# Three early expert pairs behind the first layer, and half items between the late pairs

## The chip, the cores and the metric

The kernel runs on one core of one Trainium2 chip. The time is the device time of one execution in microseconds (us). Profiled times are read from one recorded execution of the kernel. On this core TensorE (PE) does the matrix products, VectorE (DVE) and ScalarE (ACT) evict and split them, GpSimd (POOL) does some elementwise work and issues the indirect gathers and scatters, and SyncE (SP) issues all other transfers.

## What is computed

The reference is an attention, a dense two-layer network and a routed network, one after the other, on 4 x 576 = 2304 tokens of width 512:

```
attn = softmax(mask(q k^T / 8)) v          # 8 heads of 64, blocks of 64 causal
h    = x @ w_in                            # 512 -> 1024
s    = h * softmax(h);  ln = (s - mean) / sqrt(var + 1e-6) * g_ln
x    = ln @ w_out                          # 1024 -> 512
e    = argmax(x @ w_gate)                  # one expert of 8 for each token
y    = relu(x[e] @ w1[e]) @ w2[e]          # 512 -> 1024 -> 512
out  = y * softmax(x @ w_gate)[e] * sigmoid(x @ w_output_gate)[e]
```

A product that has to be as good as fp32 is made from fp16 halves: each operand is split into a high and a low part, and three products (high-high, high-low, low-high) are summed in PSUM. This is why each weight is loaded as fp32 and then split by ACT (high part, line 1370) and DVE (low part, line 1373) or POOL (lines 455 and 460).

## The kernel before, in words

The order of all instructions is written by a planner (class `Plan`). Every operation is put down with its engine, an estimated cost, the buffers and keys it reads and writes, and a priority; a lower number is more urgent. `run` then places operations one by one: for each engine it takes, among those that can start within 60 ns of the earliest, the one with the lowest priority, books buffers of a tag while it does so, and issues it. So priorities decide the order within the limits that data and free buffers set, and each engine then runs its instructions in that written order on the chip.

The attention is followed by the dense network ("layer 1", function `layer1`) in 18 tiles of 128 tokens. Tile t has priority L0 + L1 * t, so tile 16 has 96.91 and tile 17 has 101.25. Each makes its first product into the PSUM tile H (two banks, one buffer; lines 903 to 905), takes the maximum, exponential and norm (lines 917 to 948), transposes (960), makes its second product (988 to 990), writes its tokens to the DRAM tile `x2d` (1002), and makes the gate logits (1028 to 1030).

The routed network works on *items*. A *pair* is 256 tokens of one expert (two tiles of 128), a *half* is 64 tokens. There are NPAIR2 = 8 pairs, items 0 to 7, and NHALF = 5 halves, items 8 to 12; tokens that are left after these go to blocks that run only if they exist (`chain`, after everything else). An item of class `Slot` has these steps:

- `load_w`: four loads of 512 KB of the expert's w1 (line 1442, on SP) into raw buffers `w1f`. There are four of these, and w2 uses them too.
- `split_w`: eight splits into one of two buffers `w1s` (one for even, one for odd items).
- `load_x`: the token numbers (line 1420, on SP), then a gather of the tokens from `x2d` (line 1427, on POOL), one for each 128 tokens.
- `trans_x`: transposes on PE (1464) and a copy on DVE (1469) into the single buffer `gx`.
- `gemm1`, the first product: lines 1482 to 1484, 96 matmuls into the PSUM tag S (three banks), evicted by ACT (1508) and DVE (1511).
- `gemm2`, the second product: lines 1543 to 1545 for a pair, 24 matmuls for each of the two token tiles, evicted and scaled by ACT (1577) and scattered by POOL (1580); lines 1539 and 1540 for a half.

`fill_w2` loads and splits the w2 of one expert, four loads of 512 KB (line 1391). All eight experts' w2 stay in SBUF: the place of expert slot e lies over buffers of the attention and of layer 1, and can be written when those are done (`low{e}`; slot 2 lies over w_in, slot 7 over w_out). `last(j)` gives the highest expert slot that item j can belong to; the second product of item j waits for the w2 of all slots up to that one.

The first NEARLY = 2 pairs are *early*: their experts are chosen by `order` from the counts of the first EC = 14 tiles (`tab0`), while tiles 14 to 17 are still in work. All other items are chosen by `items` from all 18 tiles (`tab`), so they cannot be loaded or gathered before the last logits and the table are done. Early pairs, like all pairs, accumulate their second product in H; halves use H and A in turn. A is one PSUM bank, which the attention uses before.

The items' priorities are M0 + MJ * j with M0 = 99.05 and MJ = 14.54 for pairs, and 6 more for each half; they run in the order 0 to 12. The loads of w1 have 13 less, those of w2 12.1 less, those of x 17.5 less:

```
def pri_of(j):
    return M0 + MJ * min(j, NPAIR2) + MH * max(j - NPAIR2, 0)
```

Of the kernel before, what the change touches and what calls it, by code (L numbers as in the profile page):

```python
# [12 lines left out]
AF = mybir.ActivationFunctionType  # L13
ALU = mybir.AluOpType
# [5 lines left out]
P = 128  # L20
BLK = 64
# [163 lines left out]
def kernel(  # L185
# [15 lines left out]
    B, H, S, D = q.shape  # L201
# [17 lines left out]


    EC = 14
    NEARLY = 2
    NPAIR2 = 8
    NHALF = 5
    NITEM = NPAIR2 + NHALF
    NLATE = NPAIR2 - NEARLY
    NBLK = 10
# [6 lines left out]
    TLT = "T"  # L234
    RKT = "T"
    RP = 7.31
    TP = -0.41
    DP0 = -1.33
    DP1 = 2.98
    L0 = 27.47  # L240
    L1 = 4.34
    M0 = 99.05
    MJ = 14.54
    MH = 6.0
    MW = 13.0
    MF = 12.1
    MX = 17.5
    MT = 3.6
    FENG = ("dve", "pool", "dve", "dve")
    NPX = 2  # L250
    NPS = 3
# [56 lines left out]
    eb2 = const.tile([P, E], F32, name="eb2")  # L308
    tab0 = const.tile([1, E + 3 * NEARLY], I32, name="tab0")
    tab = const.tile([1, 4, NDYN], I32, name="tab")  # L310
# [41 lines left out]
    pln = Plan(SLK, AHEAD)  # L352
# [78 lines left out]
    op = pln.op  # L431
# [927 lines left out]
    def last(j):  # L1359
        if j < NEARLY:  # L1360
            return j
        return max(p for p in range(E) if p * (P * EC // E - BLK) <= 2 * P * j)
# [18 lines left out]
    def fill_w2(pl, e, pri):  # L1381
        ej = []
        for cc in range(F2C // 2):
            wf = Buf("w1f")
            sl = slice(2 * cc, 2 * cc + 2)

            def ld(wf=wf, cc=cc):
                if not ej:
                    ej.append(reg(tab0[0:1, e : e + 1], ET.SP, E - 1))
                src = w2[bass.ds(ej[0], 1), 2 * cc * P : (2 * cc + 2) * P, :]  # L1390
                nc.sync.dma_start(
                    out=wf.t.rearrange("p (c f) -> p c f", c=2),
                    in_=src.rearrange("o (c p) f -> p (o c) f", p=P))

            pl.op("sp", 900.0, ld, r=["top", "tab0"], w=[wf], pri=pri, lat=900.0, xfer=1456.0,
                  dly=1550.0)
            halves(
                pl, wf, lambda sl=sl: w2v[:, e, 0, sl].rearrange("p c f -> p (c f)"),
                lambda sl=sl: w2v[:, e, 1, sl].rearrange("p c f -> p (c f)"),
                ("w2", e, cc), SW2, pri, FENG[cc], [f"low{e}"])  # L1400

    class Slot:
# [121 lines left out]
            return rd + ([tab_of(self.j)] if self.j else [])  # L1524

        def gemm2(self, pl, pri):
            n, hh, hl, yp = self.n, self.hh, self.hl, Buf(self.out)
            where = []

            def mm(part, t):  # L1530
                if not where:
                    where.append(place(self.j))
                e, np_ = where[0]
                o = yp.t[:, t * 512 : (t + 1) * 512]
                ts_ = slice(t * P, (t + 1) * P)
                for f in range(2 * part, 2 * part + 2):
                    wh, wl = (w2v[:, 0:np_, a_, f, :][:, e] for a_ in range(2))
                    if n == BLK:
                        nc.tensor.matmul(o, hh.t[:, f, 0:P], wh, start=(f == 0), stop=False)
                        nc.tensor.matmul(  # L1540
                            o, hh.t[:, f, 0:P], wl, start=False, stop=(f == F2C - 1))
                        continue
                    nc.tensor.matmul(o, hh.t[:, f, ts_], wh, start=(f == 0), stop=False)  # L1543
                    nc.tensor.matmul(o, hh.t[:, f, ts_], wl, start=False, stop=False)  # L1544
                    nc.tensor.matmul(o, hl.t[:, f, ts_], wh, start=False, stop=(f == F2C - 1))  # L1545

            for t in range(self.nt):
                for part in range(4):
                    rd = self.w2_keys(part)
                    for f in range(2 * part, 2 * part + 2):  # L1550
                        rd += self.hidden(f)
                    pl.op("pe", (4 if n == BLK else 6) * c_mm(512),
                          lambda part=part, t=t: mm(part, t), r=rd, w=[(yp, t)], pri=pri)
                self.finish(pl, pri, yp, t)

        def finish(self, pl, pri, yp, t):
            y, m = self.y[t], self.m

            def scale():
                return self.ix.bitcast(F32)[0:m, t, 1:2]  # L1560

            if self.n == BLK:
                hl = self.hl

                def z():
                    return hl.t[0:BLK, 0:4].rearrange("p c t -> p (c t)").bitcast(F32)

                pl.op("act", c_act(512), lambda: nc.scalar.activation(
                    out=z(), in_=yp.t[BLK:P, 0:512], func=AF.Copy), r=[(yp, t)], w=[hl], pri=pri)
                pl.op("dve", c_dve(512), lambda: nc.vector.tensor_tensor(  # L1570
                    out=z(), in0=yp.t[0:BLK, 0:512], in1=z(), op=ALU.add), r=[(yp, t)], w=[hl],
                    pri=pri)
                pl.op("pool", c_pool(512), lambda: nc.gpsimd.tensor_scalar(
                    out=y.t[0:BLK], in0=z(), scalar1=scale(), scalar2=0.0, op0=ALU.mult,
                    op1=ALU.add), r=[hl, ("ix", self.at)], w=[y], pri=pri)
            else:
                pl.op("act", c_act(512, 1), lambda: nc.scalar.activation(  # L1577
                    out=y.t, in_=yp.t[:, t * 512 : (t + 1) * 512], func=AF.Copy, scale=scale()),
                    r=[(yp, t), ("ix", self.at)], w=[y], pri=pri)
            pl.op("pool", 1040.0, lambda: nc.gpsimd.indirect_dma_start(  # L1580
                out=out, out_offset=bass.IndirectOffsetOnAxis(
                    ap=self.ix[0:m, t, 0:1], axis=0),
                in_=y.t[0:m], in_offset=None, bounds_check=N - 1, oob_is_err=False),
                r=[y, ("ix", self.at)], w=["out"], pri=pri, lat=900.0,
                xfer=6.0 * m, dly=1690.0)
# [29 lines left out]
    for t in range(NT):  # L1615
# [3 lines left out]
        if t + 1 == EC:  # L1619
            table_consts(L0 + L1 * t - RP)  # L1620
            order(L0 + L1 * t - RP)
    items(L0 + L1 * NT + TP)
    pln.fence("top", LOW, TOP, area)
    for e in range(E):
        pln.fence(f"low{e}", e * W2E, (e + 1) * W2E, area)
    op("pool", 4000.0, lambda: [nc.gpsimd.memset(x[2], 0.0) for x in pln.tags["xg"]],
       r=["top"], w=["xgz"], pri=M0 - 10)

    def pri_of(j):
        return M0 + MJ * min(j, NPAIR2) + MH * max(j - NPAIR2, 0)  # L1630

    for e in range(E):
        fill_w2(pln, e, pri_of(next(j for j in range(NPAIR2 + 1) if last(j) >= e)) - MF)
    for j in range(NITEM):
        whole = j < NPAIR2
        sl = Slot(j, 2 * P if whole else BLK, j % 2, j,
                  "H" if whole or (j - NPAIR2) % 2 else "A")
        pri = pri_of(j)
        sl.load_w(pln, pri - MW)
        sl.split_w(pln, pri - MW)  # L1640
        sl.load_x(pln, pri - MX)
        sl.trans_x(pln, pri - MT)
        sl.gemm1(pln, pri)
        sl.gemm2(pln, pri)
    with tc.manual_schedule():
        setup_first()
        pln.run({"pool": 2000.0, "act": 1500.0, "dve": 1500.0, "sp": 500.0})
# [60 lines left out]
```

## Time and profile before

| What | Value |
|---|---|
| median of 3 runs | 781.38 us (776.32 to 785.42) |
| profiled execution | 781.41 us |
| its span, first to last instruction | 779.7 us |
| mean granted TensorE clock | 0.914 |
| PE busy | 611.7 us (78%) |
| DVE busy | 533.7 us (68%) |
| ACT busy | 367.5 us (47%) |
| POOL busy | 331.0 us (42%) |
| chain that ended last | PE 34%, DVE 29%, issue 12%, POOL 10%, DMA 9%, ACT 4% |

PE is the busiest engine, but its busy time is a mean over stages. The span has the attention up to about 410 us, with layer 1 beside it and after it up to 540 us, early pairs between 480 and 552 us, late pairs from 570 to 716 us and halves up to 764 us. The page's second part cuts the span into 40 slices of 19.5 us each, with one digit for each.

### The profile page before, as it was taken

The page shows a single profiled execution, that of the slowest core. Times are in us where ns is not written, and L with a number is a line of the kernel's source. Part 1 is how long each engine was busy: PE and PEld are TensorE (multiplying, and loading weights), DVE is VectorE, ACT ScalarE, POOL GpSimd, SP SyncE. Part 2 cuts the span into 40 slices and gives each one's busy share as a digit, 9 for nine tenths or more (in the row PEclk, how much of TensorE's full clock was granted, in tenths as well). Part 3 has the DMA queues.
Part 4 walks back from the last instruction along what each step waited for, and adds up shares of the span by engine and source line. Part 5 has one row for each costly group of instructions (what it writes and reads, how often), then busy time and mean ns, then how long its engine had stood idle before and what let it go on. Part 6 is the DMA issues. An engine that isn't in the chain of part 4 may idle for free.

```text
span 779.7 us, 14588 instructions
## 1 busy us (share of the span) xinstructions
PE 611.7 (78%) x5124; PEld 374.0 (48%) x5124; DVE 533.7 (68%) x1241; ACT 367.5 (47%) x871; POOL 331.0 (42%) x349
## 2 busy tenths in 40 slices
PE   2567767779997899897997765979269999999861
PEld 1445534434554455454553333746055667666530
DVE  6799999998997779877742746576964453234630
ACT  4558666535654555545532354556243533234510
POOL 6861757747355644535241234364442131221110
PEclk9759998979999999899998988899769999999986
DMA  8872847857988878675521167646397462343600
GB/s 208 193 203 69 177 106 163 174 130 160 206 172 145 169 161 177 131 156 85 109 52 28 27 203 260 173 162 229 110 321 240 153 207 98 132 149 136 224 9 19
DMA packets 207204, 117.46 MB, mean 151 GB/s; under 512 B 182928, under 2 KB 183056, under 8 KB 207120
## 3 DMA queue, kind: packets, MB, share of 16 engines
q1 hardware_dynamic: 203504, 106.94, 55.0%
q0 software_dynamic: 3616, 9.46, 3.3%
q8 instruction: 45, 0.74, 0.4%
q14 instruction: 39, 0.32, 0.2%
HBM read 71.49 MB, written 10.80 MB: 106 GB/s over the span
## 4 chain that ended last, share of the span: by engine, by line
PE 34%; DVE 29%; issue 12%; POOL 10%; DMA 9%; ACT 4%; SPq 0%; POOLq 0%; ACTq 0%; DVEq 0%
DVE mem L730 4%; DMA mem<-mem 4%; PE H L1543 3%; PE S L1482 3%; PE H L1545 3%; PE H L1544 3%; PE S L1484 3%; PE S L1483 3%; DVE mem L842 3%; PE S L988 2%; PE S L989 2%; PE S L990 2%; POOL mem L460 2%; DVE mem L1373 2%; DVE mem L777 2%
## 5 line engine op out<-in xcount | busy, mean ns | idle before, releaser
L1373 DVE SCALAR_TENSOR_TENSOR mem<-mem 128x1024 f16<-128x1024 f32 x76 | 99.9, 1347 | 22.6 <-ACT mem L1370 22.3
L460 POOL TENSOR_TENSOR mem<-mem 128x576 f16<-128x576 f32 (+2 forms) x70 | 104.1, 1495 | 15.5 <-ACT mem L580 8.7
L1370 ACT ACTIVATE mem<-mem 128x1024 f16<-128x1024 f32 x84 | 84.5, 1050 | 34.2 <-DMA mem<-in_moe_w_dram 28.5
L736 ACT ACTIVATE mem<-S,mem 128x512 f32<-128x512 f32 (+4 forms) x160 | 81.6, 515 | 37.1 <-DVE mem L730 26.7
L1482 PE MATMUL S<-mem 128*128 128x256 f16 (+1 forms) x416 | 85.6, 244 | 4.2 <-DVE mem L1469 3.3
L1484 PE MATMUL S<-mem 128*128 128x256 f16 (+1 forms) x416 | 85.5, 244 | 0.8 <-DVE mem L1373 0.8
L1483 PE MATMUL S<-mem 128*128 128x256 f16 (+1 forms) x416 | 85.5, 244 | 0.0
L455 POOL TENSOR_SCALAR mem<-mem 128x576 f16<-128x576 f32 (+2 forms) x65 | 54.6, 845 | 54.8 <-PE A L864 20.0
L730 DVE TENSOR_REDUCE mem<-S 128x1 f32<-128x512 f32 (+4 forms) x128 | 68.3, 543 | 5.9 <-PE S L718 3.0
L1580 POOL DMA_INDIRECT out_dram<-mem,ix x21 | 24.9, 1188 | 99.0 <-ACT mem L1577 78.7
L988 PE MATMUL S<-mem 128*128 128x512 f16 x144 | 58.0, 403 | 3.6 <-ACT mem L736 3.0
L903 PE MATMUL H<-mem 128*128 128x512 f16 x144 | 58.1, 403 | 0.7 <-DVE mem L930 0.7
L904 PE MATMUL H<-mem 128*128 128x512 f16 x144 | 58.0, 403 | 0.0
L989 PE MATMUL S<-mem 128*128 128x512 f16 x144 | 57.7, 401 | 0.0
L990 PE MATMUL S<-mem 128*128 128x512 f16 x144 | 57.4, 399 | 0.0
L905 PE MATMUL H<-mem 128*128 128x512 f16 x144 | 57.4, 398 | 0.0
L1511 DVE SCALAR_TENSOR_TENSOR mem<-S,mem 128x512 f16<-128x512 f32 x37 | 25.3, 689 | 46.4 <-ACT mem L1508 46.4
L830 PE MATMUL T<-idf,mem 128*128 128x128 f32 (+1 forms) x208 | 41.8, 304 | 16.6 <-DVE mem L842 10.1
L1543 PE MATMUL H<-mem 128*128 (+1 forms) x128 | 48.5, 379 | 7.9 <-ACT mem L1577 6.2
L715 PE MATMUL S<-mem 128*64 128x64 f16 (+4 forms) x160 | 47.4, 315 | 2.4 <-ACT mem L736 2.3
L1508 ACT ACTIVATE mem<-S 128x512 f16<-128x512 f32 x37 | 22.0, 597 | 57.8 <-PE S L1484 57.7
L1545 PE MATMUL H<-mem 128*128 (+1 forms) x128 | 48.5, 379 | 0.0
(189 smaller groups left out, 1705.5 us busy)
## 6 DMA issues: line engine op xcount, KB each, us to landing
mem<-in_moe_w_dram SPq DMA_DIRECT2D x84, 512.0 KB, 4.9
x2d<-mem SPq DMA_DIRECT2D x22, 256.0 KB, 3.1
mem<-in_q_dram SPq DMA_DIRECT2D x16, 288.0 KB, 3.5
mem<-in_k_dram SPq DMA_DIRECT2D x16, 288.0 KB, 3.9
mem<-in_v_dram SPq DMA_DIRECT2D x16, 288.0 KB, 3.6
mem<-mem SPq DMA_DIRECT2D x32, 144.0 KB, 2.9
mem<-in_moe_w_in_dram SPq DMA_DIRECT2D x8, 512.0 KB, 4.2
mem<-in_moe_w_out_dram SPq DMA_DIRECT2D x8, 512.0 KB, 4.0
```

The costliest lines, as they stand in the source:

```text
L460: nc.gpsimd.tensor_tensor(out=dst, in0=a, in1=b, op=ALU.subtract)
L730: nc.vector.tensor_reduce(out=stt.t[0:M, c : c + w], in_=src, op=ALU.max, axis=AX.X, negate=True)
L736: op("act", c_act(n, 1, 1), lambda: nc.scalar.activation(out=pexp.t[0:M, po : po + n], in_=pt.t[0:M, co : co + n], func=AF.Exp, bias=stt.t ...
L988: nc.tensor.matmul(x2p.t, lT.t[:, 0, f], wout[:, 0, f], start=(f == 0), stop=False)
L989: nc.tensor.matmul(x2p.t, lT.t[:, 0, f], wout[:, 1, f], start=False, stop=False)
L990: nc.tensor.matmul(x2p.t, lT.t[:, 1, f], wout[:, 0, f], start=False, stop=(f == FC - 1))
L1370: pl.op("act", c_act(1024, sb=1), lambda: nc.scalar.activation(out=hi(), in_=wf.t, func=AF.Copy, scale=sc), r=[wf, *x], w=[key + (0,)], pr ...
L1373: pl.op("dve", c_dve(1024), lambda: nc.vector.scalar_tensor_tensor(out=lo(), in0=wf.t, scalar=sc, in1=hi(), op0=ALU.mult, op1=ALU.subtract ...
L1482: nc.tensor.matmul(o, wh, xh, start=(c == 0), stop=False)
L1483: nc.tensor.matmul(o, wh, xl, start=False, stop=False)
L1484: nc.tensor.matmul(o, wl, xh, start=False, stop=(c == KC - 1))
L1543: nc.tensor.matmul(o, hh.t[:, f, ts_], wh, start=(f == 0), stop=False)
```

## The change

NEARLY becomes 3, so pairs 0 to 2 are early. Their second product goes to A, one bank, one token tile after the other (`yps` holds a buffer for each token tile), and no longer to H. M0 becomes 103, so that the products of all early pairs have a higher number than tile 17 of layer 1 (101.25); MJ becomes 8. The table of the late items gets a lower number (TP from -0.41 to -8). The items run in a written order, SEQ, in which the halves 8 to 11 stand in twos before the pairs 6 and 7, and half 12 comes last. The buffers `w1s` alternate along SEQ. Loads, splits and transposes get the priority of the item before (`prev`) and small offsets, in place of fixed ones.

```diff
-    NEARLY = 2
+    NEARLY = 3
...
-    TP = -0.41
+    TP = -8.0
...
-    M0 = 99.05
-    MJ = 14.54
-    MH = 6.0
-    MW = 13.0
-    MF = 12.1
-    MX = 17.5
-    MT = 3.6
+    M0 = 103.0
+    MJ = 8.0
+    MH = 3.0
+
+    SEQ = (0, 1, 2, 3, 4, 5, 8, 9, 6, 10, 11, 7, 12)
...
         def gemm2(self, pl, pri):
-            n, hh, hl, yp = self.n, self.hh, self.hl, Buf(self.out)
+            n, hh, hl = self.n, self.hh, self.hl
+            yps = [Buf(self.out) for _ in range(1 if self.out == "H" else self.nt)]
             where = []
+
+            def at(t):
+                if self.out == "H":
+                    return yps[0], slice(t * 512, (t + 1) * 512)
+                return yps[t], slice(0, 512)
...
-    def pri_of(j):
-        return M0 + MJ * min(j, NPAIR2) + MH * max(j - NPAIR2, 0)
-
+
+    at, prev = {}, {}
+    pri = M0
+    for s_, j in enumerate(SEQ):
+        at[j], prev[j] = pri, at[SEQ[s_ - 1]] if s_ else pri - MJ
+        pri += MJ if j < NPAIR2 else MH
     for e in range(E):
-        fill_w2(pln, e, pri_of(next(j for j in range(NPAIR2 + 1) if last(j) >= e)) - MF)
-    for j in range(NITEM):
+        j = next(j for j in range(NPAIR2 + 1) if last(j) >= e)
+        fill_w2(pln, e, prev[j] + 0.6)
+    for s_, j in enumerate(SEQ):
         whole = j < NPAIR2
-        sl = Slot(j, 2 * P if whole else BLK, j % 2, j,
-                  "H" if whole or (j - NPAIR2) % 2 else "A")
-        pri = pri_of(j)
-        sl.load_w(pln, pri - MW)
-        sl.split_w(pln, pri - MW)
-        sl.load_x(pln, pri - MX)
-        sl.trans_x(pln, pri - MT)
-        sl.gemm1(pln, pri)
-        sl.gemm2(pln, pri)
+        sl = Slot(j, 2 * P if whole else BLK, s_ % 2, j,
+                  "A" if j < NEARLY or not (whole or (j - NPAIR2) % 2) else "H")
+        sl.load_w(pln, prev[j] - MJ)
+        sl.split_w(pln, prev[j] + 0.3)
+        sl.load_x(pln, prev[j] - MJ)
+        sl.trans_x(pln, prev[j] + 0.2)
+        sl.gemm1(pln, at[j])
+        sl.gemm2(pln, at[j])
```

With the reference's inputs the tokens of the experts, counted from the reference in the order of the first 14 tiles, are 576, 448, 306, 206, 128, 64, 64 and 0 after 14 tiles, and 768, 512, 306, 270, 320, 64, 64 and 0 at the end.

## Rows read from the trace of the kernel before

**Rows 1.** The page's 40 slices: busy tenths of PE, its granted clock.

```profile
PE   2567767779997899897997765979269999999861
PEclk9759998979999999899998988899769999999986
```

**Rows 2.** Stretches: length, busy us of PE, PEld, DVE, ACT, POOL, clock, DMA, GB/s.

```profile
480.00:551.50 71.50, 63.18 (x429) 40.13 (x427) 47.20 (x89) 35.27 (x47) 37.50 (x28) 0.95 0.63 202
551.50:575.00 23.50, 3.60 (x32) 3.18 (x32) 18.59 (x60) 7.86 (x8) 12.97 (x10) 0.55 0.53 178
575.00:600.40 25.40, 22.81 (x150) 14.61 (x148) 15.83 (x17) 11.93 (x14) 3.40 (x4) 0.95 0.89 307
...
715.40:764.10 48.70, 38.36 (x593) 24.62 (x589) 21.66 (x25) 17.85 (x22) 8.12 (x9) 0.89 0.31 103
```

**Rows 3.** Waits of PE from 540 us: total us, times, longest.

```profile
PE T L1464 <- DMA mem<-x2d,ix: 19.9, 2, 19.0
PE A L1539 <- DVE mem L1469: 6.6, 2, 4.0
PE H L1543 <- ACT mem L1577: 5.4, 7, 0.8
PE A L1539 <- DVE mem L1511: 2.2, 1, 2.2
```

**Rows 4.** Timeline of PE, tile 17 and early pairs: start, us, instruction, [idle before].

```profile
481.85 0.27 PE L1482 MATMUL S<-mem 128*128 128x256 f16 x1
...
506.58 0.38 PE L905 MATMUL H<-mem 128*128 128x512 f16 x1
...
515.32 0.38 PE L1543 MATMUL H<-mem 128*128 128x512 f16 x1 [1.70 <-DVE mem L930]
...
522.73 0.38 PE L1543 MATMUL H<-mem 128*128 128x512 f16 x1 [0.78 <-ACT mem L1577]
...
551.12 0.38 PE L1545 MATMUL H<-mem 128*128 x1
```

**Rows 5.** Timeline, from the last logits to the first late pair.

```profile
539.95 0.17 PE L1030 MATMUL S<-wg,mem 128*128 128x16 f16 x1
...
561.09 0.20 DVE L1337 CAST tab<-mem 1x96 int32<-1x96 f32 x1
...
570.46 1.03 PE L1464 MATMUL T<-idh,mem 128*128 128x128 f16 x8 [18.96 <-DMA mem<-x2d,ix]
...
575.13 0.42 PE L1482 MATMUL S<-mem 128*128 128x256 f16 x1
```

**Rows 6.** Timeline of PE, starts of pairs 3, 5 and 6, and of pair 5's second product.

```profile
600.24 0.27 PE L1482 MATMUL S<-mem 128*128 128x256 f16 x1
...
647.17 0.27 PE L1482 MATMUL S<-mem 128*128 128x256 f16 x1 [0.34 <-DVE mem L1469]
...
657.65 0.38 PE L1543 MATMUL H<-mem 128*128 x1
...
670.33 0.27 PE L1482 MATMUL S<-mem 128*128 128x256 f16 x1 [0.33 <-DVE mem L1469]
```

**Rows 7.** Timeline of the halves: PE, and the last scatter on POOL.

```profile
729.84 0.19 PE L1482 MATMUL S<-mem 128*128 128x64 f16 x1
...
737.78 0.19 PE L1482 MATMUL S<-mem 128*128 128x64 f16 x1 [0.18 <-DVE mem L1469]
...
763.64 0.38 PE L1540 MATMUL A<-mem 128*128 x1
...
766.49 0.91 POOL L1580 DMA_INDIRECT out_dram<-mem,ix  x1 [0.28 <-POOL mem L1573]
```

**Rows 8.** Two stretches with weight loads, columns as in rows 2.

```profile
510.00:550.00 40.00, 36.75 (x239) 21.81 (x237) 28.83 (x49) 20.69 (x30) 23.03 (x16) 1.00 0.62 205
570.00:600.00 30.00, 26.01 (x175) 17.54 (x176) 20.75 (x20) 14.04 (x16) 7.93 (x6) 0.87 0.87 301
```

**Rows 9.** The page's DMA issues: times, size, median us to landing.

```profile
mem<-in_moe_w_dram SPq DMA_DIRECT2D x84, 512.0 KB, 4.9
```

More of the change, by code (lines that the diff above doesn't have):

```diff
@@ L1533, in mm @@
                 e, np_ = where[0]
-                o = yp.t[:, t * 512 : (t + 1) * 512]
+                yp, cols = at(t)
+                o = yp.t[:, cols]
                 ts_ = slice(t * P, (t + 1) * P)
@@ L1552, in gemm2, with finish @@
                     pl.op("pe", (4 if n == BLK else 6) * c_mm(512),
-                          lambda part=part, t=t: mm(part, t), r=rd, w=[(yp, t)], pri=pri)
-                self.finish(pl, pri, yp, t)
-        def finish(self, pl, pri, yp, t):
+                          lambda part=part, t=t: mm(part, t), r=rd, w=[(at(t)[0], t)], pri=pri)
+                self.finish(pl, pri, *at(t), t)
+        def finish(self, pl, pri, yp, cols, t):
             y, m = self.y[t], self.m
@@ L1568, in finish @@
                 pl.op("act", c_act(512), lambda: nc.scalar.activation(
-                    out=z(), in_=yp.t[BLK:P, 0:512], func=AF.Copy), r=[(yp, t)], w=[hl], pri=pri)
+                    out=z(), in_=yp.t[BLK:P, cols], func=AF.Copy), r=[(yp, t)], w=[hl], pri=pri)
                 pl.op("dve", c_dve(512), lambda: nc.vector.tensor_tensor(
-                    out=z(), in0=yp.t[0:BLK, 0:512], in1=z(), op=ALU.add), r=[(yp, t)], w=[hl],
+                    out=z(), in0=yp.t[0:BLK, cols], in1=z(), op=ALU.add), r=[(yp, t)], w=[hl],
                     pri=pri)
@@ L1577, in finish @@
                 pl.op("act", c_act(512, 1), lambda: nc.scalar.activation(
-                    out=y.t, in_=yp.t[:, t * 512 : (t + 1) * 512], func=AF.Copy, scale=scale()),
+                    out=y.t, in_=yp.t[:, cols], func=AF.Copy, scale=scale()),
                     r=[(yp, t), ("ix", self.at)], w=[y], pri=pri)
```

## The prediction

> **What bounds the kernel now.** I read the page's slices first [rows 1]: PE is busy for 7 to 9 tenths almost everywhere, but there is one slice of 2 late in the span, where the clock falls to 6 or 7 tenths, and a fall at the very end. The table by stages says what these are [rows 2]. Between 480 and 551.5 us PE does the tail of layer 1 and two early pairs and is 63.2 of 71.5 us busy. Then it has 3.6 us of work in 23.5 us. Then comes the first late pair, at 0.95 of the clock, and after 715.4 us the five halves take 48.7 us with 38.4 us of work. The list of PE's waits names the causes [rows 3]: 19.9 us for the gather of tokens (one wait of 19.0), and 6.6 + 2.2 us in the halves for copies and evictions that run late on DVE.
>
> The hole at 551.5 us is a chain of latencies. The last logits of tile 17 end at 539.95 + 0.17 = 540.1 us, the table of the late items is written at 561.09, the gathered tokens arrive at 570.46, the first late product starts at 575.13 [rows 5]: 35.0 us from logits to product. PE has only the rest of pair 1 to put against it, which ends at 551.12 + 0.38 = 551.5 [rows 4]. Outside this stretch and the halves, the late pairs are bound by PE alone: from pair 5 to pair 6 it is 670.33 - 647.17 = 23.16 us [rows 6], and the waits in that time are 0.78 and 0.33.
>
> **The third early pair.** It needs only the counts of 14 tiles, so its work can stand in the hole. The same work up to the end of pair 1 ends at 551.5 now; with one more pair of 23.16 us it ends at 574.7. Today the third pair ends, and pair 3 begins, at 600.24 [rows 6]. That is 600.2 - 574.7 = **-25.6**. It holds the gather wait, the half clock of pair 2's start (matmuls of 0.42 us against 0.27 [rows 5, 6]) and its waits for weights.
>
> Can the late items be ready at 574.7? Now tile 17's first product is cut in two: PE goes to pair 0 at 481.85, because 99.05 is below 101.25, and the last matmul of tile 17 ends at 506.58 + 0.38 = 507.0 [rows 4]. From there to the logits it is 33.1 us, and 35.0 to the first late product. With 103 for pair 0 the six matmuls that are missing can follow at 481.85, and the chain would end near 483 + 33 + 35 = 551. Even if nothing of this is gained it ends at 575, as now, where PE comes free. So the chain is covered with up to 23 us to spare. Against that spare go the steps moved ahead of it: one index load and four loads of 512 KB on SP, two gathers and two scatters on POOL, and eight splits (ACT and DVE). POOL is 37.5 and DVE 47.2 us busy in those 71.5 us [rows 2]; I take 0.
>
> The third pair's counts hold: its expert has 448 tokens after 14 tiles, so it is full. The five late pairs and five halves then cover the rest exactly, and the optional blocks stay empty, as now (the last scatter is at 766.49 [rows 7]).
>
> **Another accumulator.** Pair 0's second product waits 1.70 us for tile 17's eviction from H [rows 4]; in A this wait goes: **-1.7**. On the other side A has one bank, and the second token tile has to wait for the eviction of the first. With H the same wait is there, but only after six matmuls of the second tile: the product starts at 515.32 and stops at 522.73 - 0.78 = 521.95, after 30 matmuls at 0.22 us, 24 and 6 [rows 4]. Without those six it is 6 x 0.22 + 0.78 = 2.1 us. The bound is 0 to 1.3 us more for each early pair, 0 where PE has layer 1 or the first 36 matmuls of the next pair to put there, so 0 to 3.9. I take **+1.3**, for the pair at the end. The Trainium skill has a rule against this edit, in "PSUM — Partial Sum Buffer" (Summary: rules for kernel authors): while a result is read, let the matmuls write another bank. By that rule all three early pairs would pay, and the sum below would be 752.
>
> **The halves.** A half that is fed takes 737.78 - 729.84 = 7.94 us [rows 7]; five take 39.7 against 48.7 [rows 2], so 9.0 less. The weights of a half are 2 MB: at 301 GB/s [rows 8], 524288 / 301000 = 1.74 us for each of four loads, 7.0 us, which is what ties a row of halves to the loads now (waits of up to 4.0 us [rows 3]). A pair in between gives 23 us for the same loads. Two halves stand together twice, and the next item's `w1s` comes free only when the first of them has ended its first product; a wait of about half a microsecond at each of these two places I leave in. **-8.0**; bounds -9.0, and 0 if the waits only move.
>
> **The loads.** This is the unknown one. In the new numbers the w1 of item j + 1 stands ahead of the w2 that item j needs (119 against 119.6 for pair 4's w1 and slots 3 and 4). That w1 can be split only when the pair two before has ended its first product, and until then it holds all four raw buffers. A first product takes 657.65 - 647.17 = 10.5 us [rows 6], so pair 2's ends 23.2 - 10.5 = 12.7 us before 574.7, at 562. Eight loads (slots 3 and 4) follow, at 1.74 us, or at 524288 / 205000 = 2.56 us as beside layer 1 [rows 8], plus 4.9 us to land the last [rows 9], minus one load: 579 to 585. They are needed when pair 3's first product ends, 10.5 us after 574.7, at 585. Pair 4 with slots 5 and 6 repeats it 23 us later. So it just fits. Bounds: 0, and about 5 us at each of two places; I take **+2.0**.
>
> **The sum** goes against the profiled execution, 781.4 us (1.7 over its span, and equal to the median of the runs): 781.4 - 25.6 - 1.7 + 1.3 - 8.0 + 2.0 = **749.4**, so 749. The 15.7 us after the last matmul (779.7 - 764.0) stay.
>
> **The rivals.**
> - *The feed binds.* Loads go at 3.3 us in place of 2.6, since the splits on POOL are slow and DVE is shared: eight take 6 us more, at pairs 3 and 4. 749 + 12 = 761. For it: the DMA share is 0.87 to 0.89 whenever late pairs load now [rows 2, 8]. Against it: 205 GB/s is a rate that was held while layer 1 still used DVE.
> - *The hole moves.* The third pair's steps stretch layer 1's tail beyond its 23 us, or PE's written order puts something that waits before work that could run; the wait of 19 us comes back elsewhere, and the halves keep their waits: 749 + 19 + 8 = 776, no change. Against it: the chain may be as late as now at no cost.
> - *Slower: the raw buffers.* While w1 of a pair holds all four, no w2 arrives. If eight loads take more than the 23 us of a pair, every pair waits. The gain of 32 us is gone when pairs 3 and 4 wait 16 us each, with eight loads in 39 us, 4.9 us for each. At 6 us each it is two times 48 - 23 = 25, so 749 + 50 = 799. For it: the holding is in the order of priorities. Against it: no stretch of rows shows more than 2.6.
> - *Better.* Feed and halves cost nothing, and the short product waits are filled: 749.4 - 2.0 - 1.3 - 1.0 = 745, and less where layer 1's tail has fewer waits: 740.
> - *Not what it says:* a third pair that is not full would send tokens to the optional blocks, which run after everything, unhidden: half an item's 8 us, 7 of loads and a gather chain of some 10, 774. The counts exclude it for these inputs.
>
> **How the numbers follow.** Forecast 0.62; the feed 0.17; better 0.08; the hole moves 0.06; slower 0.06; optional blocks 0.01. A change under 1% (7.8 us) can't be told from none here, as the three runs span 9 us. Faster: 0.62 + 0.17 + 0.08 = 0.87; same: 0.06 + 0.01 = 0.07; slower 0.06. The range takes in the better case near its edge and the feed rival with a few us more: 738 to 767. What is left out is the other three and the tails, about 0.2.
>
> **What would show it.** PE without a gap over 3 us between 482 and the start of pair 3, with that start near 575 (the hole, right); tile 17's first product in one piece, logits near 520 (order); early second products into A with waits of at most 2.1 us; halves of about 8 us between pairs. Pair 3's or 4's second product waiting for a split of w2 by 5 us or more would show the feed; a wait of PE for a gather after the early pairs would show the hole moved. The prediction is wrong if pair 3 begins after 590, or if the items after it take more than 25 us for each pair.

## The result and the profile after

The changed kernel takes **755.35 us** (median of four runs, 753.55 to 761.62) against 782.21 us of the kernel before on the same chip: ratio 0.9679, 95% interval 0.9596 to 0.9762. The forecast was 749, with a range of 738 to 767. The recorded execution took 753.69 us, its span is 751.8 us.

The page's slices of the changed kernel, PE and its clock, answer to [rows 1]:

```profile
PE   2568858868988888989799776779899999999981
PEclk9998998698999899999999898999989999999995
```

The slice of 2 is gone, and so are the clock's 6 and 7 beside it. The stages of the changed kernel (length, busy us of PE, PEld, DVE, ACT, POOL, clock, DMA share, GB/s) answer to [rows 2]:

```profile
485.85:557.35 71.50, 61.45 (x435) 39.36 (x433) 52.97 (x142) 31.52 (x43) 31.68 (x26) 0.95 0.58 162
557.35:579.19 21.84, 21.84 (x156) 14.43 (x154) 15.61 (x16) 14.16 (x17) 8.62 (x7) 1.00 0.94 325
579.19:724.33 145.14, 137.02 (x1273) 93.78 (x1272) 80.78 (x85) 69.05 (x85) 42.05 (x36) 1.00 0.60 202
724.33:734.90 10.57, 8.27 (x113) 4.82 (x111) 0.69 (x1) 1.28 (x2) 0.98 (x1) 0.84 0.09 29
```

In the second row PE works without a pause where it had 3.6 of 23.5 us before. The third row holds five late pairs and four halves, the fourth the last half.

PE's waits from 540 us on (total us, times, longest) answer to [rows 3]:

```profile
PE H L1548 <- ACT mem L1582: 3.9, 5, 0.8
PE A L1550 <- DVE mem L1154: 2.7, 1, 2.7
PE A L1544 <- DVE mem L1509: 2.3, 1, 2.3
PE A L1550 <- DVE mem L1509: 1.6, 1, 1.6
```

The wait of 19 us for the gather is gone, and the list holds no wait for a gather at all. The timeline shows the chain that ended in it (start, us, instruction) and answers to [rows 4 to 6]:

```profile
486.93 0.38 PE L903 MATMUL H<-mem 128*128 128x512 f16 x1
...
494.75 0.27 PE L1480 MATMUL S<-mem 128*128 128x256 f16 x1
...
519.08 0.17 PE L1028 MATMUL S<-wg,mem 128*128 128x16 f16 x1
...
544.14 0.68 DVE L1509 SCALAR_TENSOR_TENSOR mem<-S,mem 128x512 f16<-128x512 f32 x1
544.74 0.23 DVE L1154 TENSOR_TENSOR mem<-mem 128x80 f32<-128x80 f32 x1
544.87 0.10 PEld L1550 LDWEIGHTS <-mem 128*128 128x128 f16 x1 [3.08 <-DVE mem L1509]
544.97 0.38 PE L1550 MATMUL A<-mem 128*128 x1 [2.68 <-DVE mem L1154]
...
549.69 0.47 DVE L1335 CAST tab<-mem 1x92 int32<-1x92 f32 x1
...
549.93 0.59 PE L1550 MATMUL A<-mem 128*128 x1 [1.56 <-DVE mem L1509]
...
579.19 0.27 PE L1480 MATMUL S<-mem 128*128 128x256 f16 x1
...
589.67 0.38 PE L1548 MATMUL H<-mem 128*128 x1
...
602.96 0.27 PE L1480 MATMUL S<-mem 128*128 128x256 f16 x1
```

Tile 17's first product ends (487.3) before pair 0's starts (494.75). The logits end at 519.25. The table is written 30.9 us later (21.2 before), and in that time DVE does eight splits of 1.22 us, 9.8 us, where before there were three, 5.6 us. PE is still at pairs 1 and 2, and pair 3 starts at 579.19, right behind pair 2.

The profile puts PE's wait of 2.68 us down to L1154, a step of the table. But that step only follows the eviction of the pair's first product on DVE (L1509, done at 544.82), and the weight load of the same matmul waits for L1509. So this wait is for the eviction, which stands behind the table's steps on DVE. The same holds for the waits put down to L1154 or to the table's last step (L1335, L1337) in the lists below.

**A common mark.** Up to tile 15 of layer 1 both kernels have the same instructions in the same order on PE. Yet the first logits matmul of tile 13 starts at 433.62 us in one recording and at 439.47 in the other:

```profile
433.62 0.18 PE L1028 MATMUL S<-wg,mem 128*128 128x16 f16 x1 [3.83 <-DMA mem<-mem]
```
```profile
439.47 0.18 PE L1026 MATMUL S<-wg,mem 128*128 128x16 f16 x1 [3.69 <-DMA mem<-mem]
```

Where this mark lies differs from recording to recording, and with the number of early pairs (last section). So stages are counted from it, and what happens ahead of it is counted apart. From it to the end of the span it is 346.1 us before and 312.3 after: **-33.8**. The median is only 26.9 lower, as the mark itself lies later in the changed kernel. From the mark to pair 3 both kernels do the same PE work (row of the kernel before, then of the changed one; columns as in the stages above):

```profile
433.62:600.24 166.62, 124.31 (x797) 75.01 (x797) 111.58 (x254) 76.74 (x101) 69.58 (x61) 0.87 0.61 197
```
```profile
439.47:579.19 139.72, 119.37 (x796) 71.84 (x797) 99.23 (x246) 67.59 (x91) 57.84 (x55) 0.94 0.62 181
```

Of the 26.9 us gained here, PE's idle time gives 22.0 (from 166.62 - 124.31 = 42.3 to 20.4), and its busy time, at a granted clock of 0.94 for 0.87, gives 4.9. The remaining 6.9 us lie behind pair 3's start.

### The profile page after: what moved, and what is told of

The parts are those of the page before. It is cut to its first block, busy times and chain, and to the rows that moved or that the text cites. A ratio compares the mean times of both kernels' runs of the same rounds, so it can differ in the third digit from the quotient of the medians.

```text
span 751.8 us, 14578 instructions
## 1 busy us (share of the span) xinstructions
PE 612.9 (82%) x5124; PEld 376.6 (50%) x5124; DVE 535.6 (71%) x1241; ACT 370.3 (49%) x871; POOL 329.7 (44%) x349
## 4 chain that ended last, share of the span: by engine, by line
PE 40%; DVE 32%; issue 9%; POOL 7%; DMA 6%; ACT 4%; POOLq 0%; SPq 0%; ACTq 0%; DVEq 0%
DVE mem L728 4%; PE S L1480 4%; PE S L1482 3%; PE S L1481 3%; DMA mem<-mem 3%; DVE mem L840 3%; DVE mem L775 3%; DVE mem L798 2%; PE H L1548 2%; PE H L1550 2%; PE H L1549 2%; DMA idxd<-pairs,pos 2%; PE S L986 2%; PE S L988 2%; PE S L987 2%
## 5 line engine op out<-in xcount | busy, mean ns | idle before, releaser
L1371 DVE SCALAR_TENSOR_TENSOR mem<-mem 128x1024 f16<-128x1024 f32 x76 | 96.5, 1299 | 21.1 <-ACT mem L1368 16.2
L458 POOL TENSOR_TENSOR mem<-mem 128x576 f16<-128x576 f32 (+2 forms) x70 | 101.7, 1459 | 16.0 <-ACT mem L578 9.0
L1585 POOL DMA_INDIRECT out_dram<-mem,ix x21 | 23.1, 1101 | 93.1 <-ACT mem L1582 62.3
L986 PE MATMUL S<-mem 128*128 128x512 f16 x144 | 56.9, 395 | 3.8 <-ACT mem L734 3.1
L988 PE MATMUL S<-mem 128*128 128x512 f16 x144 | 56.4, 391 | 2.2 <-DVE mem L965 2.2
L828 PE MATMUL T<-idf,mem 128*128 128x128 f32 (+1 forms) x208 | 44.0, 318 | 16.7 <-DVE mem L840 10.3
L987 PE MATMUL S<-mem 128*128 128x512 f16 x144 | 56.6, 393 | 0.0
L713 PE MATMUL S<-mem 128*64 128x64 f16 (+4 forms) x160 | 49.7, 329 | 2.0 <-ACT mem L734 2.0
L1509 DVE SCALAR_TENSOR_TENSOR mem<-S,mem 128x512 f16<-128x512 f32 x37 | 25.4, 688 | 35.1 <-ACT mem L1506 33.0
L714 PE MATMUL S<-mem 128*64 128x64 f16 (+4 forms) x160 | 49.8, 328 | 0.0
L836 ACT ACTIVATE mem<-T 128x512 f16<-128x512 f32 (+3 forms) x84 | 34.6, 423 | 30.6 <-PE T L828 27.4
L1506 ACT ACTIVATE mem<-S 128x512 f16<-128x512 f32 x37 | 22.0, 595 | 49.3 <-PE S L1482 42.2
## 6 DMA issues: line engine op xcount, KB each, us to landing
mem<-mem SPq DMA_DIRECT2D x32, 144.0 KB
```

The source lines that it names most:

```text
L458: nc.gpsimd.tensor_tensor(out=dst, in0=a, in1=b, op=ALU.subtract)
L986: nc.tensor.matmul(x2p.t, lT.t[:, 0, f], wout[:, 0, f], start=(f == 0), stop=False)
L987: nc.tensor.matmul(x2p.t, lT.t[:, 0, f], wout[:, 1, f], start=False, stop=False)
L988: nc.tensor.matmul(x2p.t, lT.t[:, 1, f], wout[:, 0, f], start=False, stop=(f == FC - 1))
L1371: pl.op("dve", c_dve(1024), lambda: nc.vector.scalar_tensor_tensor(out=lo(), in0=wf.t, scalar=sc, in1=hi(), op0=ALU.mult, op1=ALU.subtract ...
```

## The experiments

Ratios are to the kernel before on the same chip. The rows were timed in five sets, in which the kernel before takes 782.21 us (first two rows), 787.56 (repeated, table late, A then H), 785.40 (two early pairs, pair 0 ahead, halves last, early pairs in H), 788.23 (the four that start from the kernel before) and 784.99 (last row); so medians of different sets are not to be compared, ratios are. The stage columns are from one recording each, and the kernel before was recorded in the first set alone: mark to pair 3; PE idle within it; pair 3 to the end of the span; mark to the end of the span; mark to the end of the logits of tile 17.

| kernel | median us | ratio, 95% interval | to pair 3 | PE idle | pair 3 to end | mark to end | to logits |
|---|---|---|---|---|---|---|---|
| before | 782.21 | | 166.6 | 42.3 | 179.5 | 346.1 | 106.5 |
| changed | 755.35 | 0.9679 (0.9596 to 0.9762) | 139.7 | 20.4 | 172.6 | 312.3 | 79.8 |
| changed, repeated | 760.26 | 0.9614 (0.9539 to 0.9690) | 143.6 | 22.1 | 170.8 | 314.4 | 83.7 |
| two early pairs | 762.45 | 0.9693 (0.9643 to 0.9742) | 153.8 | 30.1 | 171.7 | 325.5 | 88.1 |
| pair 0 ahead of tile 17 | 762.02 | 0.9727 (0.9665 to 0.9789) | 148.3 | 27.1 | 169.6 | 317.9 | 103.9 |
| halves last | 756.93 | 0.9631 (0.9561 to 0.9702) | 143.2 | 21.9 | 170.7 | 313.9 | 83.5 |
| early pairs in H | 761.59 | 0.9688 (0.9638 to 0.9738) | 148.6 | 28.1 | 171.8 | 320.4 | 83.2 |
| before + third pair | 774.11 | 0.9787 (0.9723 to 0.9851) | 149.6 | 27.3 | 183.5 | 333.1 | 112.0 |
| before + order | 778.61 | 0.9859 (0.9802 to 0.9915) | 161.7 | 36.2 | 181.7 | 343.4 | 93.2 |
| before + halves' order | 782.38 | 0.9921 (0.9880 to 0.9962) | 166.8 | 43.1 | 177.3 | 344.1 | 107.0 |
| before + splits later | 774.88 | 0.9794 (0.9725 to 0.9863) | 166.7 | 44.1 | 172.3 | 339.0 | 106.9 |
| changed, table late | 757.33 | 0.9592 (0.9543 to 0.9642) | 144.0 | 25.1 | 170.2 | 314.2 | 84.6 |
| changed, A then H | 753.98 | 0.9541 (0.9486 to 0.9597) | 147.7 | 25.0 | 168.5 | 316.2 | 83.6 |
| A then H, half 12 earlier | 752.54 | 0.9599 (0.9553 to 0.9644) | 145.6 | 22.0 | 163.7 | 309.3 | 83.1 |

The ratios of the kernels that take one part out of the change (0.9631 to 0.9727) have intervals that overlap with both of the changed kernel's. So none of them is shown to be slower by its time; what they show, they show in their stages.

### How far one recording can be read: the changed kernel again

No edit.

> The changed kernel once more, for the runs beside it: pair 3 starts 139.7 us after tile 13's logits, from there to the end 172.6 us. Both within 1.5 us, if the late part is as steady as the argument needs; if single executions spread more than that, the smaller differences between the other runs say nothing.

Pair 3 started 143.6 us after the mark and not 139.7, further off than expected; pair 3 to the end is 1.8 shorter, mark to end 2.1 longer. So a difference of under 4 us at pair 3's start says nothing, nor does one of 2 us behind it.

### The third early pair, taken out and put in alone

```diff
-    NEARLY = 3
+    NEARLY = 2
```

> The changed kernel with two early pairs in place of three; all else as changed (products behind tile 17, A, halves between). Measure: the time, and in the trace the late part, from tile 13's logits to the end of the span (346.1 us before the change, 312.3 us after it), and PE's idle time between the early and the late pairs. Theory A (the third pair is what fills the hole): the early pairs end about 23 us sooner and PE then waits 12 us or more for the gather; late part 325 to 332, time about 770. Rival B (the order is what counts: with tile 17 in one piece the logits come 27 us sooner, so two pairs are cover enough): no wait over 5 us, late part 312 to 317, time within 5 us of the changed kernel's 755.

Pair 3 came 14.1 us later than in the changed kernel (10.2 later than in its repeat). The mark to the end took 325.5 us. The gather wait did not come back in one piece. PE's waits from 500 to 580 us in this kernel:

```profile
PE A L1550 <- DVE mem L1154: 5.0, 1, 5.0
PE T L1462 <- issue: 2.0, 1, 2.0
PE T L1462 <- DMA mem<-x2d,ix: 1.9, 3, 1.1
```

What is lost is seen as more idle time (30.1 us) in small pieces, and in the clock, 0.90 for 0.94. The long single wait that the theory named did not come.

The same number the other way, on the kernel before:

```diff
-    NEARLY = 2
+    NEARLY = 3
```

> The kernel before with NEARLY = 3 and nothing else: the third early pair in the old numbers, with pair 0's products ahead of tile 17, in H, halves last. Measure: start of pair 3's first product, counted from tile 13's logits (166.6 us before the change, 139.7 after it). Forecast's step (the third pair alone fills the hole): 139 to 142, late part about 320. Rival (the three parts of the early stage need each other, as undoing the order or A put the start at 148): 150 to 160, late part 330 to 340.

Pair 3 starts 17.0 us sooner after the mark than before, and what follows takes 4.0 us more. Here the loads of the late pairs show for once: pair 3's first product takes 14.9 us in place of 10.6. So the third pair is the largest single part of the stage, 10 to 17 us, but not the whole of 26.9: with two early pairs and all other edits the stage is still 166.6 - 153.8 = 12.8 us shorter than before. The two together are 29.8, near the whole. Ahead of the mark the third pair also has a price (last section).

### The order: pair 0 ahead of tile 17, or behind it

```diff
+        pj = at[j] - (3.95 if j == 0 else 0.0)
-        sl.gemm1(pln, at[j])
-        sl.gemm2(pln, at[j])
+        sl.gemm1(pln, pj)
+        sl.gemm2(pln, pj)
```

> The changed kernel with the products of pair 0 ahead of tile 17 of layer 1 again (priority 99.05, as before the change); three early pairs, A and halves as changed. Theory A (three pairs cover the chain even if it is as late as before): late part within 3 us of 312.3. Rival B (the order counts): the logits come some 20 us later and PE waits 8 to 13 us for the gather of pair 3; late part 320 to 326, time about 765.

The logits ended 103.9 us after the mark, near the 106.5 of before: without the order the logits gain almost nothing. The mark to the end took 317.9 us, between the two expectations. Pair 3 started 148.3 us after it, 8.6 later than in the changed kernel and 4.7 later than in the repeat. PE's waits from 500 to 590 us in this kernel show copies and evictions that come late on DVE beside the table's chain, in small pieces:

```profile
PE T L1462 <- DVE mem L1467: 4.7, 2, 2.7
PE A L1550 <- DVE tab L1335: 2.3, 1, 2.3
PE T L1462 <- DMA mem<-x2d,ix: 2.0, 2, 1.7
```

On the kernel before, pair 0's products alone are put behind tile 17:

```diff
+        pj = pri + (3.95 if j == 0 else 0.0)
-        sl.gemm1(pln, pri)
-        sl.gemm2(pln, pri)
+        sl.gemm1(pln, pj)
+        sl.gemm2(pln, pj)
```

> The kernel before with pair 0's products behind tile 17 (priority 103.0 in place of 99.05) and nothing else: two early pairs, H, old offsets. Forecast's step (the order only buys spare time for the chain, the hole needs work to fill it): the logits come some 20 us sooner, PE still waits 10 us or more for a gather, pair 3 starts 2 to 8 us sooner than 166.6. Rival (the hole is the late logits): the wait falls below 5 us, pair 3 starts at 150 to 155, late part 330 to 335.

The logits come 13.3 us sooner, which is half of the 26.7 of the whole change, and pair 3 only 4.9. A hole is left, now from 129.5 to 137.4 us after the mark, and PE still waits for gathers. PE's waits from 500 to 590 us:

```profile
PE T L1464 <- DMA mem<-x2d,ix: 5.0, 3, 2.8
PE H L1543 <- ACT mem L1577: 2.6, 3, 1.0
PE H L1545 <- DVE tab L1337: 2.4, 1, 2.4
```

The single wait of 19 us [rows 3] has become three of 5.0 us together. Here too the stretch is paid for in small waits.

### The accumulator of the early pairs

```diff
-                  "A" if j < NEARLY or not (whole or (j - NPAIR2) % 2) else "H")
+                  "A" if not (whole or (j - NPAIR2) % 2) else "H")
```

> The changed kernel with the early pairs' second products in H again. With tile 17 ahead in priority, H should be free when pair 0 needs it. Forecast's view (A brings 1.7 us and costs 1.3): late part within 2 us of 312.3. Rival (A is what lets pair 0's second product run beside tile 17, and so what moves the logits): tile 17's logits come 5 us or more later or pair 0's second product waits 5 us or more, late part 318 or more.

Pair 3 starts 8.9 us later than in the changed kernel, 5.0 later than in its repeat. PE's waits from 510 to 590 us in this kernel:

```profile
PE S L1480 <- DVE mem L1467: 2.9, 1, 2.9
PE H L1550 <- DVE mem L1154: 2.4, 1, 2.4
PE H L1548 <- ACT mem L1582: 2.3, 3, 0.8
```

The wait put down to L1154 is there with either accumulator, so it isn't a matter of the bank. With H each early pair pays the 0.78 us of its second token tile (three make 2.3). With A neither the changed kernel's list nor its repeat's has one of these (one wait of 1.5 us for ACT in the repeat is for an eviction of a first product, L1506).

### The table's priority

```diff
-    TP = -8.0
+    TP = -0.41
```

> The changed kernel with the table of the late items at its old, less urgent number (TP -0.41 in place of -8.0). Theory (the urgent table on DVE holds up the evictions of the early pairs, which PE waits 2.7 and 1.6 us for, while the items have time to spare): those waits go, pair 3 starts 135 to 138 us after tile 13's logits in place of 139.7. Rival (the chain has no time to spare): PE waits for a gather before pair 3, which starts at 142 or later.

The wait put down to L1154 stays (4.0 us) and pair 3 starts at 144.0, like the repeat's 143.6. This does not settle the theory. The table's number is L0 + 18 * L1 + TP, so it went from 97.59 to 105.18, which is still ahead of pairs 1 and 2 (111 and 119), and in this recording too the table's steps stand right ahead of the eviction that PE waits for. A number behind the pairs' was not tried. As pair 3 did not move, this edit is also a measure of chance, since 25.1 us of idle time stands here against 20.4 and 22.1. The order's and the accumulator's 27.1 and 28.1 are only 2 to 3 us beyond that.

### The halves: their place, or their splits

The changed kernel with the halves at the end:

```diff
-    SEQ = (0, 1, 2, 3, 4, 5, 8, 9, 6, 10, 11, 7, 12)
+    SEQ = (0, 1, 2, 3, 4, 5, 6, 7, 8, 9, 10, 11, 12)
```

> The changed kernel with the items in the order 0 to 12, so all five halves at the end. The part from the start of pair 3 to the end was 179.5 us before the change and is 172.6 now. If the halves between pairs give what was forecast: 8 us more than the changed kernel, 763, late part 320. If the halves' gain was only noise or comes from elsewhere (loads already ahead): within 2 us of 312.3.

Nothing was lost: pair 3 to the end takes 170.7 us, and five halves in a row 39.1, or 7.8 each. They need no pair between them. The other way round, the new order of items and of `w1s` on the kernel before:

```diff
+    SEQ = (0, 1, 2, 3, 4, 5, 8, 9, 6, 10, 11, 7, 12)
+    at, pri = {}, M0
+    for j in SEQ:
+        at[j] = pri
+        pri += MJ if j < NPAIR2 else MH
...
-        return M0 + MJ * min(j, NPAIR2) + MH * max(j - NPAIR2, 0)
+        return at[j]
...
-    for j in range(NITEM):
+    for s_, j in enumerate(SEQ):
...
-        sl = Slot(j, 2 * P if whole else BLK, j % 2, j,
+        sl = Slot(j, 2 * P if whole else BLK, s_ % 2, j,
```

> The kernel before with the items in the order of SEQ (halves 8 to 11 in twos before pairs 6 and 7) and the buffers w1s alternating along it; all numbers and offsets as before. Measure: from the start of pair 3 to the end of the span, 179.5 us before the change, 172.6 after it. Forecast's step (the halves' loads need a pair to hide behind): 171 to 173. Rival (what held the halves was the written order on DVE, with the four splits of the next half ahead of the evictions of this one): more than 175, with waits of PE for DVE still between the two halves of a couple.

Pair 3 to the end takes 177.3 us, 2.2 less than before, which is close to the recordings' difference. PE's waits from 671 to 765 us in this kernel show the halves waiting for evictions by DVE as much as ever, at their new places:

```profile
PE A L1539 <- DVE mem L1511: 6.4, 3, 2.7
PE H L1539 <- DVE mem L1511: 2.8, 1, 2.8
```

So I looked at what DVE does before such an eviction (L1511). DVE of the kernel before:

```profile
718.61 0.42 DVE L1469 COPY mem<-T 128x512 f16<-128x512 f16 x1 [8.23 <-PE T L1464]
719.07 4.63 DVE L1373 SCALAR_TENSOR_TENSOR mem<-mem 128x1024 f16<-128x1024 f32 x4
723.62 0.68 DVE L1511 SCALAR_TENSOR_TENSOR mem<-S,mem 128x512 f16<-128x512 f32 x1
...
738.58 5.01 DVE L1373 SCALAR_TENSOR_TENSOR mem<-mem 128x1024 f16<-128x1024 f32 x4 [0.26 <-ACT mem L1370]
743.51 0.68 DVE L1511 SCALAR_TENSOR_TENSOR mem<-S,mem 128x512 f16<-128x512 f32 x1
744.12 0.41 DVE L1469 COPY mem<-T 128x512 f16<-128x512 f16 x1
```

Four splits for the next half, 4.6 to 5.0 us, stand in DVE's order ahead of the eviction that PE needs now. In the changed kernel a split has the number of the item before plus 0.3, and so it comes behind that item's products and evictions. That one number was put alone into the kernel before, for halves 9 to 12:

```diff
+        prev = pri_of(j - 1) if j else M0 - MJ
-        sl.split_w(pln, pri - MW)
+        sl.split_w(pln, prev + 0.3 if j > NPAIR2 else pri - MW)
```

> The kernel before with one number changed for the halves 9 to 12: their weights are split behind the products of the half before (its priority and 0.3 more), not ahead of them; halves still last, loads as before. Measure: from the start of pair 3 to the end, 179.5 us before the change. Forecast's step (the halves are held by their loads): 178 to 180. Rival (the splits stand ahead of the evictions on DVE): 170 to 173, five halves in about 40 us, waits for the copy of line 1469 gone.

Pair 3 to the end takes 172.3 us, 7.2 less than before and as long as in the changed kernel. DVE in this kernel, at the first of these places:

```profile
720.42 0.42 DVE L1469 COPY mem<-T 128x512 f16<-128x512 f16 x1 [8.30 <-PE T L1464]
720.96 0.69 DVE L1511 SCALAR_TENSOR_TENSOR mem<-S,mem 128x512 f16<-128x512 f32 x1
721.90 4.63 DVE L1373 SCALAR_TENSOR_TENSOR mem<-mem 128x1024 f16<-128x1024 f32 x4 [0.26 <-ACT mem L1370]
```

The eviction now follows the copy, and the same four splits come after it. Of PE's waits from 716 to 765 us these are left:

```profile
PE S L1482 <- DVE mem L1469: 2.9, 4, 2.2
PE A L1539 <- DVE mem L1511: 1.9, 1, 1.9
```

In place of 6.6 + 2.2 us [rows 3] it is 2.9 + 1.9. With the halves in a row as good as between pairs (170.7 against 172.6) and their place alone worth 2.2, this settles the halves: the gain is the order on DVE, not their place between pairs.

### A version that could be better

Late pairs put their first token tile in A and their second in H, so that neither waits for the other's eviction:

```diff
-            yps = [Buf(self.out) for _ in range(1 if self.out == "H" else self.nt)]
+            late_pair = self.out == "H" and self.nt == 2
+            yps = [Buf(x) for x in ("A", "H")] if late_pair else [
+                Buf(self.out) for _ in range(1 if self.out == "H" else self.nt)]
...
-                if self.out == "H":
+                if self.out == "H" and not late_pair:
```

> The changed kernel with the second products of the late pairs in two accumulators, the first token tile in A and the second in H. If the 0.78 us of PE in each late pair is the wait for one tile's eviction: it goes, five times 0.78, and the part from pair 3 to the end falls from 172.6 to 168 to 170 us. Rival (the wait only moves to the next product, which needs the same evictions on ACT and DVE): 171.5 or more.

Pair 3 to the end took 168.5 us as expected. Its recorded execution took 761.4 us, the longest of its four, so its stages are weak evidence, and the pairs' pitch is read from the next kernel, which has the same edit and half 12 before pair 7 in addition:

```diff
-    SEQ = (0, 1, 2, 3, 4, 5, 8, 9, 6, 10, 11, 7, 12)
+    SEQ = (0, 1, 2, 3, 4, 5, 8, 9, 6, 10, 11, 12, 7)
```

> The changed kernel with the late pairs' second products in A and then H (as in the run before this, 168.5 us from pair 3 to the end) and with half 12 ahead of pair 7, so that a pair is last. If the wait of 1.9 us in the last half is there because nothing else is left for PE: it goes, with the half's longer end (ACT, DVE, POOL), and the part from pair 3 to the end is 165.5 to 167.5; time about 750, ratio to the kernel before 0.945 to 0.957. Rival (three halves in a row are held by their loads, 7.0 us each, and a pair at the end shows its own two evictions and scatters): 168 or more, no better than the run before.

From pair 4 to pair 5 it is 22.4 us, against 23.16, and the waits of 0.78 are gone. Pair 3 to the end takes 163.7 us, less than expected. Its ratio, 0.9599 (0.9553 to 0.9644), misses what was expected, and its interval overlaps those of the changed kernel (0.9596 to 0.9762, and repeated 0.9539 to 0.9690). Whether it is faster over all is not shown; that the stage is 7 to 9 us shorter is, in one recording.

## Why the prediction was right, step by step

**The third pair, the order and A** (-25.6 - 1.7 + 1.3 = -26.0): pair 3 starts 26.9 us sooner after the mark, 23.0 in the repeat. The sum held because it was taken as PE's work from end to end. Its shares did not, so it is in part luck that the sum came out so closely. The third pair was given nearly all; alone it gave 17.0, and without it 10.2 to 14.1 were lost. The order was priced at nothing, and taking it back cost 4.7 to 8.6; the accumulator was priced at -0.4, and taking it back cost 5.0 to 8.9. These two stand close to the spread between recordings, so their sizes stay open. Alone on the kernel before, the order gave 4.9, so that it and the third pair make 21.9 of the 23 to 27 there. What the third pair fills and what the shorter chain saves are not apart: without the third pair 12.8 of the 26.9 stayed.

**"The chain would end near 551"**: the logits came at 519.25, as the 520 forecast (the mark itself was 5.9 later than in the recording that the forecast was made from). But the table took 30.9 us from there, not 21.2, with more splits on DVE in that time (the third pair's are among them). Over the fourteen recordings this chain takes 21.2 to 22.8 us with three splits in it, 27.3 to 29.1 with four to six and 30.9 to 33.0 with seven or eight, which come together with more evictions on DVE; that the splits alone caused it was not tried. The forecast had put the steps moved ahead of the chain at 0. Pair 3's two gathers were issued at 554.6 and 556.9, and 6.3 us to land makes 563.2. Pair 3's transposes start at 573.1 and wait for nothing, with 10 us to spare where up to 23 had been counted.

**The single bank A** (+1.3): the expected wait of 2.1 us for an eviction did not come in the changed kernel; its two waits there (2.68 and 1.56) are for DVE's evictions of first products (L1509), and before the second token tile of pair 2 PE has transposes of pair 3 to do. In two of the variants an early pair does pay 0.8 us in A (once with two early pairs, twice with pair 0 ahead). The rule of the Trainium skill, "PSUM — Partial Sum Buffer" (Summary: rules for kernel authors), by which all three pairs would pay, did not decide here, as other matmuls stood between. It does decide for the late pairs, which have nothing between: with another bank for the second token tile the time from pair 4 to pair 5 falls by 23.16 - 22.4 = 0.8 us.

**The halves** (-8.0): the size is near, the reason failed. Starts of items in the changed kernel, from halves 8 and 9 on:

```profile
647.90 0.19 PE L1480 MATMUL S<-mem 128*128 128x64 f16 x1
...
664.46 0.27 PE L1480 MATMUL S<-mem 128*128 128x256 f16 x1
...
686.23 0.19 PE L1480 MATMUL S<-mem 128*128 128x64 f16 x1
...
702.56 0.27 PE L1480 MATMUL S<-mem 128*128 128x256 f16 x1
```

Halves 8 and 9 take 16.56 us, 10 and 11 take 702.56 - 686.23 = 16.33, half 12 takes 734.86 - 724.33 = 10.53, with a wait of 2.3 for an eviction and a clock of 0.84. Together 43.4, against 48.7 [rows 2]: -5.3. The five late pairs take 112.25 us in place of 115.03, -2.8, and the tail after the last matmul 16.9 in place of 15.7, +1.2. That makes the -6.9 measured, where -8.0 + 2.0 was forecast; that the size fits is luck. The failed step is "a pair in between gives 23 us for the same loads": the row of halves was not bound by loads. Without any pair between, five halves take 39.1 us, and one number on the splits moves the stage by 7.2 us. The trace of before had shown it, as PE's waits in [rows 3] were for DVE's copies and evictions, not for a weight.

**The loads** (+2.0): no such wait. In the changed kernel the second products of pairs 3, 4 and 5 start right behind the first ones (589.67 for pair 3). The feed rival is out for this kernel; it shows only where the third pair is put in alone. The hole did not move, and the raw buffers hold nobody up.

**The total**: from the mark on, -33.8 us and in the repeat -31.7, with -32.0 forecast. The medians fell by 26.9 and 27.3 and not by 32. What the sum lacks is a term ahead of the mark: the kernels with three early pairs reach it 5.7 us later on average (last section), and -32.8 + 5.7 makes -27.1. So the 749 forecast came out as 755. Put alone into the kernel before, the third pair, the order and the splits give 13.0, 2.7 and 7.1 us from the mark on, 22.8 together; the other 9 to 11 us (the loads that the third pair alone was waiting for, the accumulator, the rest of the new offsets) were not taken apart. Nor is it sure that there is such a remainder: by their medians, beside the kernel before in the same set, the same three edits give 14.1, 9.6 and 13.4 us, 37.1 together, which is more than the whole.

## What to carry to other kernels

When an engine waits out a chain of latencies, count the work that can stand there and its end against the chain's end; then also shorten the chain: here the first gave 17 us and the second 5. When PE waits for an eviction, read what the evicting engine does just before it: work for the next item, ahead of the eviction in an order that is fixed, is moved behind it by one number. Count stages from a common mark in both traces, look whether the mark itself moves between the kernels, and repeat the changed kernel once before reading differences of a few microseconds.

## What was not expected of the hardware

The same instructions in the same order on PE, up to tile 15, reach the mark at between 431.64 us (before + order) and 443.28 us (A then H), over all fourteen recordings: 11.6 us, or 1.5% of the time. Half of this goes with the number of early pairs. In the five kernels with two of them the mark lies at 431.64 to 436.34, on average at 434.5; in the nine recordings with three it lies at 433.95 to 443.28, on average at 440.2. The DMA engines tell the two sorts apart without an overlap. In the first 430 us their busy share is 0.67 or 0.68 with two early pairs and 0.72 or 0.73 with three (row of the kernel before, then of the changed one; columns as in the stages above):

```profile
0.00:430.00 430.00, 339.21 (x2944) 199.82 (x2944) 351.44 (x906) 229.38 (x691) 228.53 (x256) 0.92 0.67 144
```
```profile
0.00:430.00 430.00, 342.51 (x2918) 203.68 (x2919) 351.36 (x904) 229.96 (x690) 227.24 (x256) 0.93 0.72 144
```

The bytes are the same, 62.38 MB ahead of the mark in every recording. What takes longer are packets of 256 bytes, 171008 of them there: 21.0 to 21.3 ns each on average with two early pairs, 22.6 to 23.2 with three. Both come with the third pair alone, where it is taken out (two early pairs, 435.51) and where it is put in (before + third pair, 441.05), each beside kernels of the other sort on the same chip. One kernel with three is not later: pair 0 ahead of tile 17, at 433.95, with 22.6 ns. How a pair whose work starts behind the mark can do this was not tried. Up to the mark all fourteen recordings have the same instructions in the same order on every engine, but for the size of four small ones on POOL (IOTA and CAST) near 400 us; the tile `tab0` of the early pairs is three numbers longer, and whether that moves other buffers is not recorded. The rest of the spread is there in one and the same program (439.47 and 442.83 in the changed kernel and its repeat).

After a wait of about 5 us PE came back at half its clock. Three rows of the kernel with two early pairs (PE, behind the wait put down to L1154):

```profile
546.52 0.59 PE L1550 MATMUL A<-mem 128*128 x1 [4.98 <-DVE mem L1154]
546.90 0.63 PE L1548 MATMUL A<-mem 128*128 x1
547.33 0.63 PE L1549 MATMUL A<-mem 128*128 x1
```

These matmuls follow at 0.43 us and not at 0.22, until 551.6, so that 12 of them lose 12 x 0.21, or 2.5 us, more: here a wait cost more than its length. The granted clock is 1.00 from 530.0 to 541.5 us, with PE busy throughout, 0.84 in the wait, and 0.50, its lower level (1.2 GHz for 2.4), from 546.52 to 551.60.
